# One weight scale for both halves of the first expert, gating due with the second expert

## The chip, the cores and the metric

The kernel runs on one core of a Trainium2 chip. The metric is the device time of one execution in microseconds: 2206.57 us median of three runs (2204.44 to 2206.73) before the change. All rows below come from one execution that was profiled.

## The reference

Attention with a threshold, a gated MLP, and a mixture of eight experts follow each other on 2304 tokens of width 512. The change touches only the mixture:

```
def _moe2_ref(x, w_gate, w1, w2):           # x: 2304 x 512, 8 experts, 1024 wide
    P = np.exp(x @ w_gate - max)            # 2304 x 8
    for _ in range(8):                      # Sinkhorn
        P /= P.sum(1, keepdims=True) + 1e-09
        P /= P.sum(0, keepdims=True) + 1e-09
        P *= N / E
    for e in range(E):
        h = np.maximum(x @ w1[e], 0.0)
        out += P[:, e:e + 1] * (h @ w2[e])
```

## The kernel before

**Numbers.** Every float32 matrix is scaled by a power of two and split into two float16 parts (`split`, line 715: ScalarE copies the high part, line 717, VectorE makes the low one, line 718). A product is six matmuls a pair of blocks: high x high, high x low, low x high, over two blocks of the inner dimension. The scale of a weight needs its largest absolute value: two reductions on VectorE (line 739), a maximum over the partitions by a small matmul (line 131, `all_max`), and five small operations (`pow2_scale`).

**Tiles of the mixture.** Each expert is taken in two halves of 512 hidden columns, so there are 16 half-experts h. A half-expert multiplies by a scheme of seven products instead of eight (sums of blocks are formed first). Tokens stand in three groups g of 768; a unit u is one half-expert on one group, 48 in all. The weights of a half become seven split operands: `weight(which, h, ...)` is a generator that loads 1 MB (line 735), finds the maximum, makes the scale, forms four sums on GpSimd (line 768) and splits seven operands (lines 717, 718).

**Loop.** `first_step(c, j)` is product j (0 to 6) of chain c = 2u + f, six matmuls of 128 x 384 (line 940) into the PSUM banks X and Z, with evictions by ScalarE (`u..a`, `u..c`, `u..b`: lines 950, 957, 960) and VectorE; at j=6 GpSimd makes four sums and four low parts. `second_step` is product j for 128 token pairs, six matmuls of 128 x 256 (line 1011). A step number k counts the first steps in the order of the list `ahead`; 42 steps are a half-expert, and a chain's j=6 comes after the next chain's j=1. Second steps run 21 steps behind, three for each two first steps.

**Order.** TensorE follows the program's order in the loop (`manual_schedule`); on the other engines a planner orders instructions by an estimated time line. `behind()` makes what is issued in it stand behind the loop's last main instruction of the same engine. The generators of the weights are advanced at set steps (`due`, offsets `AT`), for half 1 from k=14 (first weights) and k=34 (second weights).

**Accumulators.** `acc[i]` holds 128 tokens of the output. Half 0 writes or adds its products unscaled, four of seven by ScalarE (line 1023), three by VectorE (1025). Later halves add `ps * coef[h]` (line 1021). `coef[h]` is the gating column times the scales of both weights and of the token. Before half 1's second steps begin, the gating must be done; then `scale_acc` multiplies the 18 accumulators by `coef[0]` (ScalarE, line 1049).

**Gating.** `logits(g)` is 60 small matmuls a group (line 854). Groups 0 and 1 are computed ahead of the last MLP group, group 2 in the loop at k=36. Then `sinkhorn()`, a generator, is advanced every third step: each part ends one column sum over the partitions (two small matmuls, line 892, `cs`) and makes the next row and column sums on VectorE (lines 884 to 897); what is left at the first second step of half 1 runs there.

**x.** The MLP's output is stored as seven operands in DRAM (`x2d`). `load_x(t)` brings operand t into one of ten buffers `xo`, by three transposing DMAs (line 809) the first time, with a store of the result to `x2s` (line 813), and by one plain load (line 815) later. The first fourteen are loaded during the MLP, the last four of them into own buffers `xs10` to `xs13`, which `logits(1)` reads. All these DMAs are on SyncE's queue. Loads in the loop are owed until the step that frees their buffer; in group 2 they are held until its logits are done.

**Start.** The weights 1 of half 0 are made during the second last MLP group. Of the weights 2 of half 0 the load, maximum and scale are there too, the sums and splits are issued just ahead of the loop (`first_w2`), since their tile lies in the pool `pc`, which opens when the MLP's tiles close. An MLP group (lines 523 to 606) has 12 pairs of matmul chains `gv` (line 530) into two PSUM banks, emptied by ScalarE and VectorE, then 72 matmuls `x` (line 561); the last one converts its result in tiles `xf` and `xh` that share the buffers `raw` and `sums` with the weights.

## Time and profile before

| what | value |
|---|---|
| median of three runs | 2206.57 us |
| the profiled execution's own time | 2203.08 us |
| its span, first to last instruction | 2201.3 us |
| mean granted TensorE clock | 0.974 |
| TensorE busy | 1966.6 us, 89% |
| VectorE, ScalarE, GpSimd busy | 73%, 59%, 60% |

PE is TensorE (PEld its weight loads), DVE VectorE, ACT ScalarE, POOL GpSimd, SP SyncE, whose q rows are DMA issues. A busy share is a mean over stages; what a stage is worth is read from its own waits. The clock has two levels; a share between them means that part of the stretch ran at the lower one.

### The profile page before, as it was taken

The page shows a single profiled execution, that of the slowest core. Times are in us where ns is not written, and L with a number is a line of the kernel's source. Part 1 is how long each engine was busy: PE and PEld are TensorE (multiplying, and loading weights), DVE is VectorE, ACT ScalarE, POOL GpSimd, SP SyncE. Part 2 cuts the span into 40 slices and gives each one's busy share as a digit, 9 for nine tenths or more (in the row PEclk, how much of TensorE's full clock was granted, in tenths as well). Part 3 has the DMA queues.
Part 4 walks back from the last instruction along what each step waited for, and adds up shares of the span by engine and source line. Part 5 has one row for each costly group of instructions (what it writes and reads, how often), then busy time and mean ns, then how long its engine had stood idle before and what let it go on. Part 6 is the DMA issues. An engine that isn't in the chain of part 4 may idle for free.

```text
span 2201.3 us, 43806 instructions
## 1 busy us (share of the span) xinstructions
PE 1966.6 (89%) x16464; PEld 1451.6 (66%) x16464; DVE 1614.1 (73%) x3424; ACT 1306.1 (59%) x2804; POOL 1324.6 (60%) x1404
## 2 busy tenths in 40 slices
PE   1358889899998979799999999999999999999998
PEld 0236667766776746577777777677677777776777
DVE  6999677777734247777778787777877787877766
ACT  6878777887743256755555555555555555555552
POOL 1247556675733266557666766776676667667754
PEclk9859899999999989899999999999999999999999
DMA  8885778877737354333343343334333333433332
GB/s 265 207 201 101 174 139 175 163 140 125 131 60 194 79 151 137 109 112 114 122 128 117 117 139 120 113 113 139 110 115 121 126 118 116 139 120 113 94 101 80
DMA packets 372612, 288.36 MB, mean 131 GB/s; under 512 B 286128, under 2 KB 299568, under 8 KB 372400
## 3 DMA queue, kind: packets, MB, share of 16 engines
q1 hardware_dynamic: 371808, 285.55, 49.8%
q8 instruction: 129, 2.11, 0.4%
q14 instruction: 83, 0.68, 0.1%
q0 software_dynamic: 64, 0.00, 0.0%
q10 hardware_dynamic: 528, 0.02, 0.0%
HBM read 193.61 MB, written 21.23 MB: 98 GB/s over the span
## 4 chain that ended last, share of the span: by engine, by line
PE 38%; DVE 15%; POOL 9%; ACT 7%; issue 3%; DMA 2%; SPq 1%; POOLq 0%; DVEq 0%; ACTq 0%
PE P L1011 17%; PE X L940 9%; PE Z L940 6%; DVE w L718 5%; PE gv L530 3%; DVE acc L1021 3%; ACT h L918 2%; PE x L561 2%; DVE h L919 1%; DVE w1m L739 1%; ACT w L717 1%; POOL h L919 1%; DVE w2m L739 1%; DMA xo<-x2d 1%; DVE h L969 1%
## 5 line engine op out<-in xcount | busy, mean ns | idle before, releaser
L1011 PE MATMUL P<-w,h 128*128 128x256 f16 x6048 | 771.2, 273 | 11.0 <-DVE w1mx L133 6.3
L1011 PEld LDWEIGHTS <-h 128*128 128x128 f16 x6048 | 591.8, 98 | 151.6 <-issue 16.2
L940 PEld LDWEIGHTS <-w 128*128 128x128 f16 x4032 | 396.4, 98 | 258.7 <-issue 69.9
L1021 DVE SCALAR_TENSOR_TENSOR acc<-P,coef,acc 128x256 f32<-128x256 f32 x945 | 441.5, 477 | 126.0 <-PE P L1011 116.2
L940 PE MATMUL X<-xo,w 128*128 128x384 f16 x2304 | 441.4, 329 | 53.1 <-ACT u9c L957 7.0
L940 PE MATMUL Z<-xo,w 128*128 128x384 f16 x1728 | 328.8, 327 | 0.0
L304 POOL TENSOR_TENSOR hl<-e,hl 128x512 f16<-128x512 f32 x144 | 171.9, 1193 | 229.6 <-ACT hl L303 150.0
L530 PE MATMUL gv<-xnT,wg 128*128 128x256 f16 x1296 | 168.1, 278 | 8.3 <-DVE u L540 7.1
L530 PE MATMUL gv<-xnT,wv 128*128 128x256 f16 x1296 | 167.8, 276 | 0.0
L330 PE MATMUL pv<-vs,eT 128*128 128x64 f16 (+1 forms) x2240 | 102.9, 201 | 49.7 <-DMA eT<-hl 46.2
L561 PE MATMUL x<-wo,tT 128*128 128x512 f16 x648 | 144.4, 379 | 0.9 <-DVE u L540 0.9
L530 PEld LDWEIGHTS <-wg 128*128 128x128 f16 x1296 | 125.8, 100 | 28.8 <-issue 9.5
L330 PEld LDWEIGHTS <-eT 128*128 128x128 f16 (+1 forms) x2240 | 90.8, 106 | 77.3 <-DMA eT<-hl 60.0
L298 DVE SCALAR_TENSOR_TENSOR e<-S,nt,e 128x576 f32<-128x576 f32 x144 | 116.5, 810 | 32.7 <-ACT e L296 32.3
L530 PEld LDWEIGHTS <-wv 128*128 128x128 f16 x1296 | 126.8, 99 | 16.1 <-issue 0.2
L292 DVE TENSOR_REDUCE nt<-S 128x1 f32<-128x576 f32 x144 | 106.9, 750 | 30.5 <-PE S L282 29.8
L545 POOL TENSOR_TENSOR tT<-u,tT 128x256 f16<-128x256 f32 x108 | 74.3, 689 | 79.6 <-ACT tT L544 79.4
L296 ACT ACTIVATE e<-S,nt,c 128x576 f32<-128x576 f32 x144 | 117.7, 819 | 0.3 <-issue 0.3
L561 PEld LDWEIGHTS <-tT 128*128 128x128 f16 x648 | 62.1, 98 | 71.6 <-issue 1.2
L303 ACT ACTIVATE hl<-e 128x576 f16<-128x576 f32 x144 | 97.1, 676 | 16.1 <-DVE e L298 9.6
L539 DVE SCALAR_TENSOR_TENSOR u<-u,gv 128x256 f32<-128x256 f32 x108 | 44.9, 415 | 76.0 <-ACT u L538 68.9
L282 PE MATMUL S<-kT,qT 128*128 128x288 f16 (+1 forms) x320 | 65.6, 312 | 33.6 <-DVE e L298 24.5
(2539 smaller groups left out, 3607.4 us busy)
## 6 DMA issues: line engine op xcount, KB each, us to landing
xo<-x2s SPq DMA_DIRECT2D x319, 384.0 KB, 3.1
w1r<-in_moe_w_dram SPq DMA_DIRECT2D x16, 1024.0 KB, 5.0
w2r<-in_moe_w_dram SPq DMA_DIRECT2D x16, 1024.0 KB, 5.5
x2s<-xo SPq DMA_DIRECT2D x17, 384.0 KB, 2.7
wgatew<-in_moe_w_gate_dram SPq DMA_DIRECT2D x12, 512.0 KB, 6.0
wo<-in_moe_w_out_dram SPq DMA_DIRECT2D x12, 512.0 KB, 4.1
wvalw<-in_moe_w_val_dram SPq DMA_DIRECT2D x12, 512.0 KB, 4.4
x2d<-xs SPq DMA_DIRECT2D x24, 256.0 KB, 2.8
```

The lines of the kernel that those rows point to most:

```text
L292: V.tensor_reduce(mx, sv, AX.XY, ALU.max)
L296: A.activation(ev, sv, AF.Exp, bias=nt[:, 0:1], scale=st["c2"][:, c : c + 1])
L298: V.scalar_tensor_tensor(ev, sv, nt[:, 1:2], ev, ALU.is_ge, ALU.mult, accum_out=sums[:, slot : slot + 1])
L303: A.activation(hl[:, 0:S], e, AF.Copy)
L304: G.tensor_tensor(hl[:, S + REM :], e[:, 0 : NCH * P], hl[:, 0 : NCH * P], ALU.subtract)
L330: T.matmul(o, lhsT=a, rhs=r, start=n == 0, stop=n == len(mm) - 1)
L530: T.matmul(gv[:, a, :], lhsT=w[:, l, kk, f * P : (f + 1) * P], rhs=xt[:, r * KD + kk, :], start=n == 0, stop=n == 3 * KD - 1,)
L561: T.matmul(ps, lhsT=tT[f][:, l, o : o + P], rhs=wo[:, f, r, :], start=n == 0, stop=n == 3 * KF - 1,)
L718: V.scalar_tensor_tensor(dst[1], src, s, dst[0], ALU.mult, ALU.subtract)
L940: T.matmul(ps, lhsT=w[:, a, l, kk, f * P : (f + 1) * P], rhs=xb[:, r * 2 + kk, :], start=n == 0 and j in (0, 1, 3), stop=n == 5, skip_grou ...
L1011: T.matmul(ps, lhsT=hs[u, ao, f][:, l, jj * P : (jj + 1) * P], rhs=w2[h][:, bo, r, f, :], start=n == 0 and j in (0, 1, 3), stop=n == 5, sk ...
L1021: main[True] = V.scalar_tensor_tensor(y, ps, coef[h][:, i : i + 1], y, ALU.mult, ALU.add)
```

## The change

- Both halves of the first expert get one scale for the first weights and one for the second, from the larger maximum of the two halves. Half 1's weights are loaded once more for that, ahead of the loop, and reduced whole. In the loop half 1 skips its maximum (four empty parts keep the times of the rest).
- With one scale, half 1 adds its products to the accumulators unscaled on VectorE. Coefficients, `scale_acc` and the end of the gating move from the start of half 1's second steps to that of half 2's. `scale_acc` is issued in `behind()`.
- The gating's parts come every sixth step instead of every third.
- All three `logits` are in the loop, at the j=6 of each group's first chain; loads owed are held in each group until its logits are done. The last four early x operands go through three shared buffers `xs` and only to DRAM.
- The second weights of half 0 are made whole ahead of the last MLP group's instructions, in the pool `pb`; second weights of even halves lie in `pb`, of odd ones in `pc`, one buffer each (before: two in `pc`).

```diff
-    def weight(which, h, pool, bufs=1):
+    def load_w(which, h):
         ...
         nc.sync.dma_start(out=r, in_=src.rearrange("(k p) f -> p k f", p=P))
+        return r
+    def largest(dst, r):
+        V.tensor_reduce(dst, r, AX.XY, ALU.max, apply_absolute_value=True)
+    def scale(which, h, m):
+        bits = 3 if which == 1 else 8
+        return pow2_scale(all_max(m, f"w{which}mx"), 1, bits, f"w{which}_{h % 3}")
+    def weight(which, h, pool, r=None):
+        r = load_w(which, h) if r is None else r
         yield
-        m = small([P, 2], f"w{which}m", bufs=2)
-        for a in range(2):
-            V.tensor_reduce(
-                m[:, a : a + 1], r[:, 2 * a : 2 * a + 2], AX.XY, ALU.max,
-                apply_absolute_value=True,
-            )
+        if h >= 2:
+            m = small([P, 2], f"w{which}m", bufs=2)
+            for a in range(2):
+                largest(m[:, a : a + 1], r[:, 2 * a : 2 * a + 2])
+                yield
+            V.tensor_tensor(m[:, 0:1], m[:, 0:1], m[:, 1:2], ALU.max)
             yield
-        V.tensor_tensor(m[:, 0:1], m[:, 0:1], m[:, 1:2], ALU.max)
-        yield
-        ...
+            s, inv = scale(which, h, m[:, 0:1])
+            yield
+        else:
+            s, inv = joint[which]
+            for _ in range(4):
+                yield
...
-    for _ in weight(1, 0, lambda: pb):
-        pass
-    first_w2 = weight(2, 0, lambda: pc, 2)
-    for _ in range(5):
-        next(first_w2)
+    joint = {}
+    for which in (1, 2):
+        m = small([P, 2], f"w{which}m", bufs=2)
+        r = load_w(which, 1)
+        largest(m[:, 1:2], r)
+        r = load_w(which, 0)
+        largest(m[:, 0:1], r)
+        V.tensor_tensor(m[:, 0:1], m[:, 0:1], m[:, 1:2], ALU.max)
+        joint[which] = scale(which, 0, m[:, 0:1])
+        for _ in weight(which, 0, lambda: pb, r=r):
+            pass
...
-            xb = pool.tile([P, KX, TW], F16, tag=f"xs{t}", name=f"xs{u}_{op}")
+            xb = pool.tile([P, KX, TW], F16, tag="xs", name=f"xs{u}_{op}", bufs=3)
...
-    logits(0)
-    logits(1)
...
-        if h > 0:
+        if h > 1:
             main[True] = V.scalar_tensor_tensor(y, ps, coef[h][:, i : i + 1], y, ALU.mult, ALU.add)
-        elif j in (0, 2, 3, 6):
-            A.activation(y, ps, AF.Copy)
+        elif h == 0 and j in (0, 2, 3, 6):
+            main["A"] = A.activation(y, ps, AF.Copy)
         else:
-            V.tensor_tensor(y, ps, y, ALU.add)
+            main[True] = V.tensor_tensor(y, ps, y, ALU.add)
...
-            A.activation(acc[i], acc[i], AF.Copy, scale=coef[0][:, i : i + 1])
+            with behind():
+                main["A"] = A.activation(acc[i], acc[i], AF.Copy, scale=coef[0][:, i : i + 1])
...
-    for _ in first_w2:
-        pass
...
-            if h == 0 and f == 0 and j == 6 and g == NGR - 1:
+            if h == 0 and f == 0 and j == 6:
                 logits(g)
                 gated = u
-            if h != 0 or g < NGR - 1 or gated == u:
+            if h > 0 or gated >= k // 14:
...
-            elif steps is not None and (k - started) % 3 == 0:
+            elif steps is not None and (k - started) % 6 == 0:
...
-                    if hh == 1:
+                    if hh == 2:
...
-                    if hh > 0:
+                    if hh > 1:
                         coef[hh] = coefs(hh)
-                if j == 0 and u // NGR == 1:
+                if j == 0 and u // NGR == 2:
                     m = u * NJ + jj + 1
-                    if m // NJ // NGR == 1:
+                    if m // NJ // NGR == 2:
                         scale_acc(m // NJ, m % NJ)
```

## Rows read from the trace of the kernel before

**Rows 1.** Busy time by stretch: stretch, its us, busy us (instructions) of engines, clock.

```profile
650.00:778.00 128.00, 119.11 (x932) 83.96 (x931) 44.00 (x117) 38.36 (x81) 39.89 (x50) 0.97 0.49 124
778.00:814.20 36.20, 22.98 (x115) 12.40 (x114) 15.25 (x28) 19.05 (x41) 25.68 (x25) 0.81 0.63 161
814.20:1053.36 239.16, 216.25 (x1658) 159.24 (x1656) 180.14 (x386) 142.91 (x306) 153.90 (x147) 0.97 0.40 122
1053.36:1226.25 172.89, 166.58 (x1267) 123.52 (x1265) 134.68 (x267) 94.58 (x196) 117.89 (x112) 1.00 0.39 121
```

**Rows 2.** TensorE's waits, 777 to 935: who for whom, us, times, longest.

```profile
PE cs L892 <- DVE skc L889: 8.4, 3, 5.6
...
PE cs L892 <- DVE acc L1025: 2.6, 1, 2.6
PE P L1011 <- DVE w1mx L133: 1.3, 2, 0.9
```

**Rows 3.** Timeline of TensorE: start, us, what, [idle time before, releaser].

```profile
783.99 5.50 PE L940 MATMUL X<-xo,w 128*128 128x384 f16 x18 [3.93 <-ACT u0c L957]
...
809.83 4.54 PE L940 MATMUL X<-xo,w 128*128 128x384 f16 x18 [6.89 <-ACT u2c L957]
...
920.61 1.14 PE L940 MATMUL X<-xo,w 128*128 128x384 f16 x6
921.58 0.82 PE L1011 MATMUL P<-w,h 128*128 128x256 f16 x6
...
931.65 2.08 PE L940 MATMUL X<-xo,w 128*128 128x384 f16 x6 [6.96 <-ACT u9c L957]
```

**Rows 4.** Groups by line, 784 to 1000: busy us, mean ns, idle before.

```profile
L1021 DVE SCALAR_TENSOR_TENSOR acc<-P,coef,acc 128x256 f32<-128x256 f32 x54 | 25.3, 478 | 9.8 <-PE P L1011 8.0 <-ACT acc L1049 1.0
...
L1049 ACT ACTIVATE acc<-acc,coef 128x512 f32<-128x512 f32 x18 | 11.3, 708 | 0.0
L1025 DVE TENSOR_TENSOR acc<-P,acc 128x256 f32<-128x256 f32 x27 | 11.0, 412 | 0.9 <-PE P L1011 0.6
...
L854 PE MATMUL logits<-wg,xo 128*128 128x16 f16 x60 | 1.7, 169 | 0.0
```

**Rows 5.** Groups of VectorE by line, 848 to 935: gating, first and last.

```profile
L887 DVE TENSOR_TENSOR lg<-lg,skr 128x144 f32<-128x144 f32 x8 | 4.8, 600 | 0.1
...
L894 DVE TENSOR_SCALAR ski<-cs 128x8 f32<-128x8 f32 x8 | 1.3, 159 | 2.4 <-PE cs L892 2.4
```

**Rows 6.** Timeline of GpSimd and ScalarE, 806 to 809.

```profile
806.32 1.57 POOL L768 TENSOR_TENSOR w2s<-w2r,w2s 128x512 f32<-128x512 f32 x1
...
807.93 0.72 ACT L717 ACTIVATE w<-w2s,w_s 128x512 f16<-128x512 f32 x1 [1.91 <-POOL w2s L768]
```

**Rows 7.** Groups by line of VectorE, 650 to 784: weights of half 0.

```profile
L718 DVE SCALAR_TENSOR_TENSOR w<-w1r,w_s,w 128x512 f16<-128x512 f32 x4 | 4.2, 1100 | 0.3 <-ACT w L717 0.3
L718 DVE SCALAR_TENSOR_TENSOR w<-w1s,w_s,w 128x512 f16<-128x512 f32 x3 | 3.9, 1339 | 0.0
...
L739 DVE TENSOR_REDUCE w1m<-w1r 128x1 f32<-128x1024 f32 x2 | 2.3, 1216 | 3.5 <-DMA w1r<-in_moe_w_dram 3.5
...
L718 DVE SCALAR_TENSOR_TENSOR w<-w2r,w_s,w 128x512 f16<-128x512 f32 x3 | 2.2, 746 | 0.3 <-issue 0.3
```

**Rows 8.** Timeline of TensorE in the last MLP groups: three waits.

```profile
680.54 0.55 PE L854 MATMUL logits<-wg,xo 128*128 128x16 f16 x16 [2.44 <-DVE wg L837]
...
689.23 2.06 PE L530 MATMUL gv<-xnT,wg 128*128 128x256 f16 x12 [2.50 <-DVE u L540]
...
731.06 0.27 PE L854 MATMUL logits<-wg,xs 128*128 128x16 f16 x4 [2.01 <-DMA xs<-x2d]
```

**Rows 9.** Timeline of SyncE's queue: transposing loads of group 2, first and last.

```profile
795.81 5.79 SPq L809 DMA_TRANSPOSE xo<-x2d  x4
...
830.00 2.54 SPq L809 DMA_TRANSPOSE xo<-x2d  x2
```

**Rows 10.** DMA issues, 655 to 740: count, median us to landing.

```profile
xo<-x2d SPq DMA_TRANSPOSE x30, 3.0
```

More of the change, by code (lines that the diff above doesn't have):

```diff
@@ L735, in weight @@
         nc.sync.dma_start(out=r, in_=src.rearrange("(k p) f -> p k f", p=P))
-        yield
-        m = small([P, 2], f"w{which}m", bufs=2)
-        for a in range(2):
-            V.tensor_reduce(
-                m[:, a : a + 1], r[:, 2 * a : 2 * a + 2], AX.XY, ALU.max,
-                apply_absolute_value=True,
-            )
-            yield
-        V.tensor_tensor(m[:, 0:1], m[:, 0:1], m[:, 1:2], ALU.max)
-        yield
-        bits = 3 if which == 1 else 8
-        s, inv = pow2_scale(all_max(m[:, 0:1], f"w{which}mx"), 1, bits, f"w{which}_{h % 3}")
-        yield
+        return r
[6 more added lines that the diff above has]
+        r = load_w(which, h) if r is None else r
+        yield
+        if h >= 2:
[4 more added lines that the diff above has]
+            V.tensor_tensor(m[:, 0:1], m[:, 0:1], m[:, 1:2], ALU.max)
+            yield
+            s, inv = scale(which, h, m[:, 0:1])
[4 more added lines that the diff above has]
+                yield
         sm = pb.tile([P, 7, HD], F32, tag="sums", name=f"w{which}s{h}")
@@ L769, in weight @@
             yield
-        w = pool().tile([P, NOP, 2, 2, HF], F16, tag=f"w{which}", name=f"w{which}_{h}", bufs=bufs)
+        w = pool().tile([P, NOP, 2, 2, HF], F16, tag=f"w{which}", name=f"w{which}_{h}")
         for o, a in enumerate((*parts, sm[:, 0], sm[:, 1], sm[:, 2])):
@@ L778, with w_pool @@
     w1, w2, inv1, inv2 = {}, {}, {}, {}
-    def w1_pool(h):
+    def w_pool(h):
         return pb if h % 2 == 0 else pc
-    for _ in weight(1, 0, lambda: pb):
-        pass
-    first_w2 = weight(2, 0, lambda: pc, 2)
-    for _ in range(5):
-        next(first_w2)
+    joint = {}
[9 more added lines that the diff above has]
+            pass
     ORDER = ((0, 0, 0), (1, 1, 1), (2, 5, 4), (3, 4, 2), (4, 3, 5), (5, 2, 6), (6, 6, 3))
@@ L792 @@
     XUSE = [ORDER[j][2] for j in (0, 1, 2, 3, 4, 5, 6)]
-    saved = {}
+    saved = set()
     def load_x(t, pool=None):
@@ L818, in load_x @@
         else:
-            saved[t] = xb
+            saved.add(t)
     pt_cm = tc.tile_pool(name="pt", bufs=1, side="left", reuse_waits="tile")
@@ L827, in x_of @@
         t = u * NOP + XUSE.index(op)
-        return xop[t] if t in xop else saved[t]
+        return xop[t]
     gr = small([P, KD, E], "gr")
@@ L1063 @@
         for which, base in ((1, 42 * (hn - 1) + 14 * (hn == 1)), (2, 42 * (hn - 1) + 21 + 13 * (hn == 1))):
-            n = weight(which, hn, (lambda p: lambda: p)(w1_pool(hn) if which == 1 else pc), which)
+            n = weight(which, hn, (lambda p: lambda: p)(w_pool(hn)))
             for x in AT:
```

## The prediction

> **What bounds the kernel now.** I read the page first (TensorE 89% busy, VectorE 73%, the others about 60%), then the busy time by stretch, then TensorE's waits, then the timelines at the places those two point to. The stretches [rows 1] cut the program at first-step numbers k, counted from the trace: k=2 starts at 778.0 us, k=21 at 814.2, k=126 at 1053.4, k=210 at 1226.2. The last stretch is the steady state: 84 steps in 172.89 us, 2.058 us a step, TensorE idle for 172.89 - 166.58 = 6.3 us. It runs like this to the end, so a change there would count thirteen times over; nothing in the diff alters a step from k=168 (fifth half-expert) on. What can move lies in three earlier stretches.
>
> - Loop, k=21 to 126: 239.16 us for 105 steps, where the steady rate gives 105 x 2.058 = 216.1. Loss 23.0. Named waits of TensorE: 8.4 + 2.6 us for the gating's column sums (`cs`, line 892) and 1.3 for the weight maxima [rows 2], 7.0 for `u9c` on ScalarE [rows 3].
> - Start, k=2 to 21: 36.20 us for 19 steps. A step at full clock starts 0.97 us after the last one (920.61 and 921.58 in [rows 3]), so 18.5 would do. Loss 17.7: 36.20 - 22.98 = 13.2 idle (3.9 for `u0c`, 6.9 for `u2c` [rows 3], 2.4 in shorter ones), the rest the clock: granted 0.81 in this stretch, so part of it at the lower of the two levels (1.2 and 2.4 GHz), and after those two waits 18 matmuls took 5.50 and 4.54 us where three steps need 3.1.
> - MLP, 650 to 778: 128.00 us, TensorE idle 8.9, among it 2.5 at 689 and 2.0 at 731 [rows 1, 8], each with slow matmuls behind it.
>
> **The change, part by part.**
>
> *Gating later and sparser (loop).* Sinkhorn's nine line groups on VectorE sum to 25.1 us for 8 rounds, 3.14 a round ([rows 5] has the first and the last of the nine). One part now comes each 3 steps, 6.2 us at the steady rate. The rest of VectorE's work is (134.68 / 84) = 1.60 us a step [rows 1], 4.8 in three: 4.8 + 3.1 = 7.9 us of work in 6.2 us. That is why TensorE waits at `cs`. With a part every 6 steps there are 12.4 us for 9.6 + 3.1 = 12.7; but between k=36 and 90 the second steps are still those of halves 0 and 1. For half 0 three of seven evictions are on VectorE at 412 ns, against seven at 478 [rows 4], saving 1.5 x (7 x 0.478 - 3 x 0.412)/7 = 0.45 us a step, 2.7 in six. That leaves 10.0 in 12.4 up to k=62, and with the cheaper add of half 1 (412 for 478 ns, 0.6 in six steps) 12.1 in 12.4 after it, less the maxima that are gone. It fits, narrowly in the second part. I let 3 of the 11.0 us of `cs` waits stand: -8.0 (ends: 0, as nothing but the spacing changes, and -11.0). What is late next is an eviction on VectorE, in that 3.
>
> *Scaling of the first expert's sums.* The 18 scalings take 11.3 us of ScalarE [rows 4] and ran as one block after the coefficients were ready; `u9c` stood behind them, 7.0 us. Now they come in half 2, a pair per 128 tokens, each queued behind ScalarE's last loop instruction. ScalarE is at 94.58 of 172.89 us there [rows 1]; a pair of 1.4 us every 9.6 us raises its share from 55 to 69%. Behind a scaling on ScalarE stand evictions of X, for which TensorE waits: I charge 1.5 us for the 18. -7.0 + 1.5 = -5.5 (ends -7.0 and +4: each of nine pairs in the way for its 1.4 us, 12.6, less 7.0, rounded down for what overlaps). The clock behind the two long waits: six matmuls took 2.08 us at 931.65 for 1.14 [rows 3], and some neighbours are as slow; I work with 2.0 to 2.5 us each, -4.5 (ends -6 and 0).
>
> *One scale for both halves.* In the loop the two reductions each of weights 1 and 2 of half 1 and the two maxima over partitions go: 1.3 us of TensorE's wait and 4 x 1.2 us of VectorE (counted above). -1.3.
>
> *Logits of groups 0 and 1* move into the loop: 60 small matmuls each, 1.5 us net a piece (the 1.7 of [rows 4] overlaps its neighbours by a little): +1.5 here, +1.5 in the start. When the big waits go, the steady state's own short ones (6.3 in 84 steps) show in k=21 to 84, where there are now few: +2.
>
> Loop: -8.0 - 5.5 - 4.5 - 1.3 + 1.5 + 2 = -15.8; I take -14, since three items lean on one VectorE estimate.
>
> *Second weights of half 0 (start).* Four sums on GpSimd, and the splits, run inside the start: the last sum ends at 807.9, ScalarE sits 1.91 us for it, then copies, and `u2c`, for which TensorE waits until 809.8, comes behind that [rows 3, 6]. All of that goes into the MLP stretch. GpSimd still has eight operations a chain, so ScalarE still waits for it at times: I leave 2 of 6.9 us, and 0.5 of the 1.5 us of clock behind it; of the 3.9 us for `u0c` 1.2 go, because three splits of 0.75 us stand among VectorE's work at 779 to 781 (the 746 ns in [rows 7]). -4.9 - 1.0 - 1.2 + 1.5 for logits = -5.6 (ends -12, if ScalarE never waits, and +3, if the chain only moves its wait to GpSimd's other eight).
>
> *What the MLP stretch takes on.* Whole-tile reductions of half 1 (two, at 2 x 1.2 us each [rows 7], 4.8 us of VectorE), two more loads of 1 MB, seven splits of weight 2 on VectorE less the three that are in [rows 7], four sums on GpSimd. The stretch has idle room (VectorE 44, ScalarE 38, GpSimd 40 us of 128 [rows 1]), but a matmul group there needs its bank back from VectorE, and seven splits in a row hold VectorE for 8.1 us. In the present trace such a row (672 to 680) held TensorE 2.4 us (680.5 in [rows 8]); I charge 3 for a second and 3.5 for the longer reductions. Off go the logits of two groups (1.7 each, as in [rows 4]) and the wait at 731 with its clock (2.0 + 2.0), which was a transposing load that logits needed early. +6.5 - 3.4 - 4.0 = -0.9 (ends: -8, if VectorE's additions hide, and +14, if 4.8 + 9.4 us of them are exposed whole).
>
> The trace has splits of 746 ns beside an idle GpSimd, and 1100 to 1339 ns while it works [rows 7]. The Trainium skill (SBUF — State Buffer, Who interferes with whom) says that a VectorE instruction with two SBUF inputs and a GpSimd instruction that reads SBUF exclude each other, and the loser stands for the whole of the other; this speaks against moving splits under MLP work that has GpSimd busy. By that rule each of seven splits could wait for a whole sum of 1.3 us, 14 us in place of my 8.1, and the total would be 6 us worse; the trace agrees in kind, with about 0.4 to 0.6 us a split.
>
> *Loads held back.* Loads into x buffers now wait for each group's logits, so five of the seven transposed x tiles of group 2 start at k=22 or just after. Issuing seven took from 795.8 to 832.5 [rows 9], 5.2 us each with the weight loads between, and a transposing load lands 3.0 us after its issue [rows 10]. Five from about 806 are issued by 832 and there by 835; the last is needed at k=36, 806 + 14 x 2.06 = 835. No charge, but no slack (ends 0 and +7, one late tile and the clock). Pools: the second weights alternate between two pools of one buffer, as deep as two buffers in one. 0.
>
> **Sum.** -14 - 5.6 - 0.9 = -20.5. The profiled execution took 2203.08 us (span 2201.3 and 1.8 around it): 2182.6. It lies 3.5 under the median of the runs shown, 2206.57, and the median is what is timed again: about 2186.
>
> **Rivals.**
> - *All covered.* ScalarE and VectorE have room everywhere, no `cs` wait is left and the start runs near TensorE's rate: loop -15.8 - 3 - 1.5 = -20.3, start -5.6 - 2.5 = -8.1, MLP -4, together -32: 2174. For it: no engine but TensorE is over 80% in any stretch of [rows 1]. Against: the queues are in order and these waits came at averages below 80%.
> - *MLP exposed.* The weight work stands whole in the MLP groups: +14 in place of -0.9 leaves -5.6: 2201. For it: the rows of 672 to 680 and the 2.5 us at 689. Against: that stretch has VectorE idle for 84 of 128 us.
> - *Late x tiles*: the transposes held to k=22 run 5 to 7 us late at k=36: 2192. For it the missing slack; against it, a faster start leaves the queue empty earlier.
> - *Not where it says.* The second weights' load waits for a staging buffer that the first weights free, and the x conversion of the last group takes the same buffers; if the splits still land after 778, the start keeps its 17.7 and gains nothing: 2192 to 2196.
> - *Scalings late: slower.* In half 2 each of nine pairs of scalings precedes VectorE's first add of its 128 tokens. VectorE's queue is in order: if the add waits for its pair, 1.4 us [rows 4], the evictions of Z behind it wait, and TensorE with them. With as much again until VectorE has worked off what queued up, and 0.4 of slow clock, that is 3.2 us a pair and 28.8 for nine; it decides from (20.5 + 1.5) / 9 = 2.4 us a pair, and gives 2213. Against it: all but the first pair are issued 128 tokens ahead, some 9.6 us.
>
> **How the numbers follow.** Forecast 0.56, all covered 0.13, MLP exposed 0.14, late x tiles 0.05, not where it says 0.05, scalings late 0.07. A measurement of this kernel tells about 0.2%, 4.4 us, from no change. Within it fall 0.04 of MLP exposed, 0.01 of the weights that stay, 0.02 of late scalings: 0.07. Slower: 0.05 and 0.01 of MLP exposed with a slow clock on top: 0.06. Faster: 0.87. The ends of the terms add up to -42 and +30, but do not come together; 2170 to 2205 leaves out some 0.05 below (all covered, at its far end) and 0.12 above.
>
> **What would show it.** Steps: k=21 to 126 in about 225 us; waits of `cs` for VectorE at most 3 us and none over 2; no block of scalings; k=2 to 21 in about 31 us with no wait of 6 us; the steady stretch at 172.9 us; the stretch before k=2 as long as now, within some 8 us. Wrong: a `cs` wait as large as now (VectorE's load, not spacing, was the cause), a new wait for `xo` at k=30 to 36, waits of `gv` for VectorE in a row in the last MLP group, or a steady stretch that differs at all.

## The result, and the profile after

The changed kernel takes 2182.69 us (median; 2178.03 to 2184.43) against 2205.63 for the kernel before, run beside it on the same chip: a ratio of 0.9893, 95% interval 0.9875 to 0.9911. Measured twice more beside other kernels it came to 0.9901 both times. Its profiled execution took 2184.43 us (span 2182.7) at a granted clock of 0.979, 18.65 us less than the one of before. The forecast was 2186 for the median, and -20.5 between the profiled executions.

The first view is the busy time by stretch of the changed kernel, cut at the same steps as [rows 1] (k=2 is now at 784.3 us, k=21 at 808.2, k=126 at 1034.6).

```profile
650.00:784.00 134.00, 123.80 (x841) 85.82 (x840) 52.33 (x125) 41.79 (x86) 43.98 (x55) 0.92 0.56 142
784.30:808.20 23.90, 20.67 (x176) 12.62 (x175) 10.19 (x22) 16.81 (x38) 18.96 (x21) 1.00 0.67 169
808.20:1034.60 226.40, 214.00 (x1716) 159.56 (x1715) 171.10 (x367) 137.52 (x299) 154.88 (x147) 0.99 0.44 132
1034.60:1208.00 173.40, 166.49 (x1267) 123.51 (x1265) 134.58 (x267) 98.91 (x204) 118.20 (x112) 1.00 0.38 121
```

Read against [rows 1]: the start fell from 36.2 to 23.9 us, the loop from 239.2 to 226.4, the steady stretch stayed nearly (172.9 and 173.4; eight of the 18 scalings, 5.3 us of ScalarE, now lie behind k=126), and the stretch ahead of k=2 grew. A cut at fixed times misleads there, so that stretch is cut at the first matmul of its last two MLP groups:

| stretch | before | after | difference |
|---|---|---|---|
| start of the program to the last MLP group but one | 665.8 | 669.2 | +3.4 |
| last MLP group but one | 60.1 | 68.1 | +8.0 |
| last MLP group, to k=2 | 52.1 | 47.0 | -5.1 |
| start, k=2 to 21 | 36.3 | 23.9 | -12.4 |
| loop, k=21 to 126 | 239.15 | 226.4 | -12.75 |
| k=126 to the end | 1147.9 | 1148.1 | +0.2 |

The first line is not put down to the change: over all the profiled executions below that stretch ended anywhere from 665.5 to 672.3 us (672.1 in a kernel whose only edit lies at k=36 and later), and from 640 us to its end TensorE works without a gap at full clock before and after.

TensorE's waits of the changed kernel follow: who waits for whom, us, times, longest. First the loop (808 to 1035), which answers to [rows 2]:

```profile
PE P L1030 <- DVE w1mx L133: 4.3, 2, 3.1
PE P L1030 <- DVE acc L1044: 2.5, 5, 1.0
PE P L1030 <- DVE ski L913: 2.1, 2, 1.1
PE X L959 <- ACT u11b L979: 1.2, 1, 1.2
PE cs L911 <- DVE acc L1044: 1.2, 1, 1.2
PE X L959 <- ACT u17b L979: 1.0, 1, 1.0
```

The waits of `cs` fell from 11.0 us to 1.2, and the 7.0 for `u9c` [rows 3] is gone. The 2.1 us of `P` for `ski` are new: `ski` is the gating's, and its first instruction empties the PSUM bank of a column sum, which a second step takes next. At the top stands a wait for the weight maximum, 4.3 us in the loop where it was 1.7 (1.3 of it up to 935 us, [rows 2]). Next the start (784 to 808) and the MLP (655 to 784):

```profile
...
PE X L959 <- ACT u1c L976: 1.0, 1, 1.0
...
PE gv L530 <- DVE u L540: 8.3, 3, 3.7
PE w1mxp L131 <- DVE xm L570: 1.9, 1, 1.9
```

**The start**, in TensorE's timeline; the rows answer to 783.99 and 809.83 of [rows 3].

```profile
786.62 3.08 PE L959 MATMUL X<-xo,w 128*128 128x384 f16 x18 [0.23 <-ACT u0c L976]
...
805.17 3.16 PE L959 MATMUL X<-xo,w 128*128 128x384 f16 x18 [2.02 <-ACT u2c L976]
```

The wait for `u0c` went from 3.93 to 0.23 us and the 18 matmuls behind it from 5.50 to 3.08; `u2c` went from 6.89 to 2.02 and from 4.54 to 3.16.

**The last MLP group but one**, TensorE's timeline. A `gv` chain of 12 takes 1.47 us where nothing disturbs it.

```profile
688.62 2.72 PE L530 MATMUL gv<-xnT,wg 128*128 128x256 f16 x12 [3.19 <-DVE u L540]
691.14 2.77 PE L530 MATMUL gv<-xnT,wv 128*128 128x256 f16 x12
...
705.86 2.72 PE L530 MATMUL gv<-xnT,wg 128*128 128x256 f16 x12 [3.66 <-DVE u L540]
```

Two chains after each wait run at about half speed, at the lower of the clock's two levels (granted 0.50 from 688.62 to 693.70 and from 705.86 to 710.90, 0.85 in the group on the mean). VectorE's timeline shows what TensorE's banks waited for:

```profile
681.87 3.72 DVE L718 SCALAR_TENSOR_TENSOR w<-w1r,w_s,w 128x512 f16<-128x512 f32 x4
685.52 2.06 DVE L718 SCALAR_TENSOR_TENSOR w<-w1s,w_s,w 128x512 f16<-128x512 f32 x3
688.17 0.74 DVE L540 SCALAR_TENSOR_TENSOR u<-u,gv 128x256 f32<-128x256 f32 x2
```

Seven splits in a row hold VectorE from 681.87 to 687.58; the evictions `u`, which free a bank, stand behind them in the queue, and TensorE starts again at 688.62. The same happens at 699 to 705 with the second weights' seven. The third wait for `u` (1.4 us) and the one for `xm` (1.9) lie at 672 to 675.5 us, behind the first weights' whole-tile reductions.

**The new wait in the loop**, TensorE and then VectorE:

```profile
966.41 0.22 PE L131 MATMUL w1mxp<-ident,w1m 128*128 128x128 bf16 x1
969.77 1.66 PE L1030 MATMUL P<-w,h 128*128 128x256 f16 x12 [3.14 <-DVE w1mx L133]
```

```profile
965.16 0.29 DVE L916 TENSOR_TENSOR lg<-lg,ski 128x144 f32<-128x144 f32 x1
...
966.64 1.92 DVE L925 TENSOR_SCALAR coef<-lg,w_i 128x18 f32<-128x18 f32 x2
...
969.44 0.28 DVE L133 TENSOR_REDUCE w1mx<-w1mxp 128x1 f32<-128x128 f32 x1
```

The small matmul of the maximum of weights 1 of half 3 is done at 966.63. The reduction of its result stands on VectorE behind the coefficients of two half-experts, and the next second step on TensorE waits for its bank. The program issues these coefficients at the first second step of half 2 (k=105); VectorE has them earlier, right behind the gating's last instruction at 965.16. With a part every sixth step that last part is issued at k=90, next to the maximum of half 3, which is due at k=94.

### The profile page after: what moved, and what is told of

Its sections match the earlier page's. It is cut to its first block, busy times and chain, and to the rows that moved or that the text cites. A ratio compares the mean times of both kernels' runs of the same rounds, so it can differ in the third digit from the quotient of the medians.

```text
span 2182.7 us, 43793 instructions
## 1 busy us (share of the span) xinstructions
PE 1967.9 (90%) x16462; PEld 1453.4 (67%) x16462; DVE 1606.6 (74%) x3404; ACT 1305.3 (60%) x2804; POOL 1321.1 (61%) x1404
## 4 chain that ended last, share of the span: by engine, by line
PE 42%; DVE 16%; POOL 8%; ACT 7%; issue 4%; DMA 1%; SPq 0%; DVEq 0%; POOLq 0%; ACTq 0%
PE P L1030 17%; PE X L959 9%; PE Z L959 6%; PE gv L530 5%; DVE w L718 5%; PE x L561 3%; DVE acc L1040 3%; ACT h L937 2%; ACT w L717 2%; DVE h L938 2%; DVE w1m L740 1%; POOL h L938 1%; DVE w2m L740 1%; DVE h L988 1%; DMA eT<-hl 1%
## 5 line engine op out<-in xcount | busy, mean ns | idle before, releaser
L1030 PEld LDWEIGHTS <-h 128*128 128x128 f16 x6048 | 591.2, 98 | 157.6 <-issue 22.9
L1040 DVE SCALAR_TENSOR_TENSOR acc<-P,coef,acc 128x256 f32<-128x256 f32 x882 | 411.8, 477 | 113.3 <-PE P L1030 105.4
L530 PEld LDWEIGHTS <-wg 128*128 128x128 f16 x1296 | 128.7, 101 | 36.4 <-issue 14.4
L296 ACT ACTIVATE e<-S,nt,c 128x576 f32<-128x576 f32 x144 | 117.7, 819 | 0.3 <-issue 0.3
L282 PE MATMUL S<-kT,qT 128*128 128x288 f16 (+1 forms) x320 | 66.3, 314 | 33.0 <-DVE e L298 23.7
```

What stands on the lines that cost most here:

```text
L296: A.activation(ev, sv, AF.Exp, bias=nt[:, 0:1], scale=st["c2"][:, c : c + 1])
L530: T.matmul(gv[:, a, :], lhsT=w[:, l, kk, f * P : (f + 1) * P], rhs=xt[:, r * KD + kk, :], start=n == 0, stop=n == 3 * KD - 1,)
L1030: T.matmul(ps, lhsT=hs[u, ao, f][:, l, jj * P : (jj + 1) * P], rhs=w2[h][:, bo, r, f, :], start=n == 0 and j in (0, 1, 3), stop=n == 5, sk ...
L1040: main[True] = V.scalar_tensor_tensor(y, ps, coef[h][:, i : i + 1], y, ALU.mult, ALU.add)
```

## The experiments

All ratios are to the kernel before, run on the same chip, with 95% intervals. The last four columns, in us, are from each profiled execution.

| kernel | ratio | MLP group but one | last group | start | loop |
|---|---|---|---|---|---|
| before | 1 | 60.1 | 52.1 | 36.3 | 239.2 |
| changed | 0.9893 [0.9875, 0.9911] | 68.1 | 47.0 | 23.9 | 226.4 |
| e_after2 | 0.9901 [0.9881, 0.9921] | 65.6 | 52.1 | 25.5 | 226.4 |
| e_after3 | 0.9901 [0.9884, 0.9919] | 65.5 | 48.7 | 25.5 | 226.5 |
| e1_every3 | 0.9939 [0.9926, 0.9951] | 66.3 | 52.1 | 25.5 | 231.0 |
| e3_block | 0.9937 [0.9923, 0.9950] | 65.0 | 48.7 | 23.9 | 231.3 |
| e5_before6 | 1.0036 [1.0022, 1.0051] | 59.8 | 53.5 | 36.4 | 246.9 |
| e2_w2_late | 0.9917 [0.9904, 0.9930] | 60.4 | 53.3 | 29.5 | 224.8 |
| e10_three | 0.9891 [0.9874, 0.9907] | 64.4 | 48.5 | 27.3 | 224.7 |
| e6_no_half1 | 0.9885 [0.9867, 0.9902] | 62.3 | 53.2 | 23.9 | 228.0 |
| e4_spread | 0.9912 [0.9899, 0.9926] | 56.2 | 59.3 | 23.9 | 227.4 |
| e7_spread2 | 0.9885 [0.9868, 0.9901] | 56.4 | 54.1 | 25.5 | 224.8 |
| e8_store | 0.9881 [0.9863, 0.9899] | 64.0 | 47.0 | 25.5 | 224.8 |
| e9_both | 0.9827 [0.9809, 0.9845] | 49.1 | 47.1 | 23.9 | 226.5 |

**The loop: spacing (e1_every3).** The changed kernel with the old spacing of the gating's parts.

```diff
-            elif steps is not None and (k - started) % 6 == 0:
+            elif steps is not None and (k - started) % 3 == 0:
```

> The changed kernel with the gating's parts every third step again; they are still due only with half 2. Theory (the spacing removed the column-sum waits): the waits of cs for VectorE come back to some 8 to 11 us with a slow clock behind, k=21 to 126 takes 235 to 238 us for 226.4, time about 2193 against 2182.7. Rival (the waits came from half 1's maxima and the deadline, not from the spacing): cs waits stay under 3 us and the time within 3 us of 2182.7.

TensorE's waits in its loop:

```profile
PE cs L911 <- DVE skc L908: 7.8, 2, 6.6
PE cs L911 <- DVE acc L1044: 2.5, 1, 2.5
```

The waits of [rows 2] are back almost to the figure (10.3 us against 11.0), and the ratio rises to 0.9939. So these waits came from the spacing, with all else as in the changed kernel. But the loop is only 4.6 us longer, where 9 to 12 were expected: with the wide spacing go waits that it brings, 2.6 us for `w1mx`, 2.1 for `ski` and 2.3 for `acc`. TensorE's idle time rises by 1.8 us, and its busy time by 2.8 at a granted clock of 0.97 for 0.99. The spacing is worth 4.6 us of the loop, not the 9.1 by which `cs` differs.

This run also says what makes the new wait for `w1mx`; VectorE and TensorE:

```profile
941.65 1.06 DVE L925 TENSOR_SCALAR coef<-lg,w_i 128x18 f32<-128x18 f32 x1
```

```profile
982.53 1.47 PE L1030 MATMUL P<-w,h 128*128 128x256 f16 x12 [0.38 <-DVE w1mx L133]
```

Here the gating is through at 922 us, the coefficients run at 924 to 943, and the maximum of half 3, at 982, costs 0.38 us in place of 3.14. So it is the end of the gating, moved by the spacing, that puts them in its way.

**The loop: the deadline (e5_before6).** The reverse: the kernel before with the wide spacing alone.

```diff
-            elif steps is not None and (k - started) % 3 == 0:
+            elif steps is not None and (k - started) % 6 == 0:
```

> The kernel before with one thing changed: parts of the weight work are let out at every sixth step and not at every third, each half's scale and due time left as they were. Theory (the wide spacing is open only because the gating and scaling are due with the second expert, so that the parts have 40 steps more): here the parts left over at the end of the first expert's steps run in one lump ahead of its first matmuls of the second layer, TensorE waits there for several us, and the loop k = 21 to 126 is longer than the 239.2 us of before by 5 to 30 us; median 2211 to 2235. Rival (spacing alone brings the gain, as e1_every3, which took it away, cost 9 us): the waits of cs for skc go (8.4 us) and the loop takes 230 to 233; median 2197 to 2200.

The "parts of the weight work" of this expectation are the gating's parts, as the edit shows. The kernel is slower than before, and its loop 7.7 us longer. TensorE's timeline at the point where half 1's second steps begin:

```profile
914.84 0.59 PE L892 MATMUL cs<-skc,ones 128*128 128x8 f32 x2 [4.73 <-DVE skc L889]
...
930.34 0.60 PE L892 MATMUL cs<-skc,ones 128*128 128x8 f32 x2 [2.67 <-DVE skc L889]
```

The five rounds left over run in one lump, 17.8 us of waits. So the one scale, which costs reductions and a load, earns its place here by moving the due time; the spacing can't be had without it.

**The loop: order of the scalings (e3_block).** They are issued where they were, not behind the loop's own ScalarE work.

```diff
-            with behind():
-                main["A"] = A.activation(acc[i], acc[i], AF.Copy, scale=coef[0][:, i : i + 1])
+            A.activation(acc[i], acc[i], AF.Copy, scale=coef[0][:, i : i + 1])
```

> The changed kernel with the 18 scalings issued without an order behind the loop's instructions. Theory (the order kept them from running as one block): they run in blocks of 3 to 6 us on ScalarE near k=104 to 110, one wait of TensorE of 5 to 8 us with slow clock behind: 7 to 9 us slower, about 2191. Rival (with the coefficients known early the planner spreads them itself): no wait over 2 us, time within 3 us of 2182.7.

ScalarE's timeline, and the wait that it makes for TensorE:

```profile
968.06 6.25 ACT L1068 ACTIVATE acc<-acc,coef 128x512 f32<-128x512 f32 x10 [2.22 <-DVE coef L926]
```

```profile
PE X L959 <- ACT u13b L979: 3.7, 1, 3.7
```

The block is back, and an eviction behind it holds TensorE 3.7 us, in the place of `u9c`'s 7.0 (5 to 8 were expected). The loop is 4.9 us longer than the changed one. So the move to half 2 alone takes the wait from 7.0 to 3.7 us, and the place in the queue takes the rest.

**The start: sums and four splits (e2_w2_late).** The generator of the second weights of half 0 is made ahead of the last MLP group and run only ahead of the loop. The three splits that need no sum went into the MLP by themselves (699.5 to 701.8 us), since their tile is in `pb`.

```diff
-        for _ in weight(which, 0, lambda: pb, r=r):
-            pass
+        half0 = weight(which, 0, lambda: pb, r=r)
+        if which == 1:
+            for _ in half0:
+                pass
...
+    for _ in half0:
+        pass
     BEHIND = 7
```

> The changed kernel with the sums and splits of half 0's second weights issued after the last MLP group, just ahead of the loop, as before; tile still in pb. Theory (ScalarE stood behind GpSimd's sums in the start, and the MLP stretch pays for the move): k=2 to 21 takes 34 to 37 us for 23.9, the MLP stretch gets 4 to 6 us shorter; net 6 to 9 us slower, about 2190. Rival (the start got faster for other reasons: logits gone, coefficients gone): k=2 to 21 stays under 27 us and the time falls to about 2178.

TensorE's waits in its start, then a sum on GpSimd and ScalarE's queue ahead of `u2c`:

```profile
PE X L961 <- ACT u2c L978: 5.6, 1, 5.6
...
PE X L961 <- ACT u0c L978: 0.2, 1, 0.2
```

```profile
805.07 1.57 POOL L783 TENSOR_TENSOR w2s<-w2r,w2s 128x512 f32<-128x512 f32 x1
```

```profile
806.68 0.72 ACT L717 ACTIVATE w<-w2s,w_s 128x512 f16<-128x512 f32 x1 [0.81 <-POOL w2s L783]
808.08 0.52 ACT L939 ACTIVATE h<-u1s 128x384 f16<-128x384 f32 x1 [0.67 <-POOL u1s L997]
808.51 0.47 ACT L978 ACTIVATE u2c<-X 128x384 f32<-128x384 f32 x1
```

The wait for `u2c` is back (5.6 us, before 6.9): ScalarE stands for the sums and for what runs behind them on GpSimd, and `u2c` behind that. The wait for `u0c` is not back. The start takes 29.5 us, 5.6 above the first profiled execution of the changed kernel (4.0 above the other two) and 6.8 below before. That is between the theory's 34 to 37 us and the rival's 27: this part of the second weights explains a third to a half of the start's gain. The MLP group but one takes 60.4 us, where three executions of the changed kernel take 65.5 to 68.1. But the last group takes 53.3, with a wait of 3.2 us for `u`, so both together (113.7 us for 114.2 to 117.7) don't price the move.

**The start: the three splits (e10_three).** Now only those three are put back on VectorE ahead of `u0a`, where they stood.

```diff
-        for o, a in enumerate((*parts, sm[:, 0], sm[:, 1], sm[:, 2])):
+        todo = list(enumerate((*parts, sm[:, 0], sm[:, 1], sm[:, 2])))
+        if which == 2 and h == 0:
+            todo = [todo[o] for o in (1, 4, 5, 6, 0, 2, 3)]   # the last three wait
+        for o, a in todo:
...
+    with tc.issue_after(places["V"].ins):      # the last reduction of the last MLP group
+        for _ in half0:
+            pass
...
-            V.tensor_tensor(st["A"], Z, st["A"], ALU.add)
+            with tc.issue_after(places["split"].ins) if (u, f) == (0, 0) else ExitStack():
+                V.tensor_tensor(st["A"], Z, st["A"], ALU.add)
```

> The changed kernel with one thing put back: the low parts of the three second-weight splits of half 0 that need no sum stand on VectorE just ahead of the addition u0a, where they stood in the kernel before (779 to 781 us there). The sums and the other four splits stay in the MLP groups. Theory (these three hold up u0a, hence ScalarE's u0c, for which TensorE waits at a lowered clock): the wait of X for u0c is back at 2 to 4 us with slow matmuls behind it, u2c waits no more than 2 us, and k = 2 to 21 takes 28 to 32 us against 23.9 to 25.5; the loop stays at 225 to 228. Rival (the 1.2 us that the prediction charged for them is all they cost, and the rest of the start's gain has another cause, as the logits or the loads that left it): 25 to 26.7 us, with no wait for u0c over 1.5 us. The total, 2181 to 2193, can't tell the two apart.

27.3 us, short of the theory's 28 to 32 and over the rival's 26.7, and no wait for `u0c`. ScalarE's order differs; first the kernel before, then this one:

```profile
782.05 0.52 ACT L953 ACTIVATE u0a<-u0a 128x384 f32<-128x384 f32 x1 [6.38 <-DVE u0a L952]
782.48 0.67 ACT L581 ACTIVATE xf<-x,xm 128x512 f32<-128x512 f32 x1
783.05 0.51 ACT L918 ACTIVATE h<-u0a 128x384 f16<-128x384 f32 x1
783.46 0.48 ACT L957 ACTIVATE u0c<-X 128x384 f32<-128x384 f32 x1
```

```profile
781.88 0.49 ACT L986 ACTIVATE u0c<-X 128x384 f32<-128x384 f32 x1 [5.28 <-PE X L968]
784.08 0.52 ACT L982 ACTIVATE u0a<-u0a 128x384 f32<-128x384 f32 x1 [1.71 <-DVE u0a L981]
...
793.56 0.52 ACT L946 ACTIVATE h<-u0s 128x384 f16<-128x384 f32 x1 [2.66 <-POOL u0s L1005]
793.99 0.47 ACT L986 ACTIVATE u1c<-X 128x384 f32<-128x384 f32 x1
```

Before, ScalarE's relu of `u0a` waited for VectorE's add behind the three splits, and `u0c` stood fourth in that queue. Here `u0c` stands ahead of that relu; the conversion of the last group's x slipped instead, GpSimd's sums with it, and TensorE waited 2.93 us for `u1c`, with 18 matmuls of 4.54 us behind. Against the changed kernel's 23.9 to 25.5 us the three splits cost 1.8 to 3.4 us here, about their own 2.1 us and not clearly more. What they cost in the old order this run can't say, and the theory is not shown.

**MLP: is it the look at half 1? (e6_no_half1).** Its two loads and reductions are left out; the scales come from half 0 alone, so this kernel leaves out half 1's part of the maxima.

```diff
-        r = load_w(which, 1)
-        largest(m[:, 1:2], r)
...
-        V.tensor_tensor(m[:, 0:1], m[:, 0:1], m[:, 1:2], ALU.max)
```

> The changed kernel without the look at half 1 ahead of the loop: both scales come from half 0's maximum alone, so two loads of 1 MB and two whole-tile reductions are left out. Theory (the last but one MLP group pays for VectorE's longer work): that group falls from 68 to 62 to 64 us, time 4 to 6 us under the changed kernel's. Rival (the splits in rows are the price, not the reductions): the group stays at 66 to 68 us, time within 2 us.

62.3 us in the group but one, 3 to 6 less than the changed kernel's three executions, and a total (0.9885) that the intervals don't tell from 0.9893. The group came out as the theory said, but the 4 to 6 us in the total did not show. The price of looking at half 1 is small, and this run can't give it better.

**MLP: weights among the groups' own work (e4_spread, e7_spread2).** Each reduction (in halves) and each split is bound behind the work of one of the group's 12 matmul pairs, the first weights in the last group but one and the second in the last. In e4_spread the second weights' loads are issued just ahead of the last group, in e7_spread2 a group earlier.

```diff
+    def put(n, j, f):          # one part of the weights behind pair f of group j
+        with ExitStack() as es:
+            for ins in places[j, f]:
+                es.enter_context(tc.issue_after(ins.ins))
+            next(n, None)
...
+    for f in range(KF):
+        put(n1, LASTJ - 1, f)
+    next(n2)                   # e7_spread2: the loads; e4_spread has this line further down
...
-    mlp_out(NTL // 2 - 1, mlp_in(NTL // 2 - 1), pb)
+    tT8 = mlp_in(LASTJ, lambda f: put(n2, LASTJ, f))
```

> The changed kernel with half 0's weights spread: reductions in halves, one part behind each of the 12 pairs of matmul chains, the first weights in the last but one MLP group, the second in the last. Theory (the MLP stretch loses to rows of splits that hold VectorE while matmuls wait for their banks): the waits of gv for VectorE, 8.3 us, shrink under 2, slow clock goes, the last but one group falls from 52.5 to 35 to 42 us: 10 to 15 us faster than the changed kernel, 2168 to 2173. Rival (the stretch is set by its DMA queue, on which the stores and transposes stand in one line): the group stays over 48 us and the time within 4 us of 2182.7.

> As e4_spread, but the second weights' loads are issued ahead of the x loads, so that no reduction stands in VectorE's queue for a load. Theory (rows of splits and a late load were the price): the 9.65 us wait goes, no wait of gv over 4.1 us is left, both groups together 104 to 110 us where the changed kernel took 115; time 2170 to 2176. Rival (stores of x behind transposing loads on SyncE's queue set these groups): waits of 3 to 4 us with ScalarE standing for a store stay in both groups, together 112 to 116 us, time 2180 to 2186.

The group but one fell to 56 us in both, not to the 35 to 42 expected. And in e4_spread a load came late, so that the last group took 59.3 us; SyncE's queue, VectorE and TensorE:

```profile
733.01 1.07 SPq L740 DMA_DIRECT2D w2r<-in_moe_w_dram  x2
```

```profile
738.88 1.22 DVE L745 TENSOR_REDUCE w2m<-w2r 128x1 f32<-128x1024 f32 x1 [11.40 <-DMA w2r<-in_moe_w_dram]
```

```profile
740.94 2.72 PE L532 MATMUL gv<-xnT,wg 128*128 128x256 f16 x12 [9.65 <-DVE u L542]
```

The loads stood behind transposing loads on SyncE's queue, the reduction waited in VectorE's queue with the evictions behind it, and TensorE 9.65 us. With the loads earlier that is gone, and both groups together take 110.5 us, where the theory said 104 to 110 and the rival 112 to 116. A second mechanism shows; e7_spread2, ScalarE, then SyncE's queue, then TensorE:

```profile
688.32 0.42 ACT L605 ACTIVATE xs<-x2t 128x256 f16<-128x256 f32 x1 [5.98 <-DMA x2d<-xs]
```

```profile
684.57 1.23 SPq L861 DMA_TRANSPOSE xo<-x2d  x1
685.89 0.52 SPq L607 DMA_DIRECT2D x2d<-xs  x1
```

```profile
690.06 2.72 PE L532 MATMUL gv<-xnT,wg 128*128 128x256 f16 x12 [4.42 <-DVE u L542]
```

ScalarE's copy into `xs` waits for the store that empties the buffer, the store stands behind the transposing loads, and the next `gv` eviction stands behind the copy.

**MLP: the stores by another queue (e8_store).** The stores of `x2d` of two groups are issued by GpSimd.

```diff
-            nc.sync.dma_start(
+            (G if j in (NTL // 2 - 3, NTL // 2 - 2) else nc.sync).dma_start(
```

> The changed kernel with the x stores of the two MLP groups before the last issued from GpSimd's queue instead of SyncE's, where they stand behind transposing loads. Theory (rows of splits are the price in the last but one group): that group stays over 62 us, and only the wait in the last group, where there is one, goes: time 2178 to 2184. Rival (the queue sets both groups): the last but one group falls under 60 us and the time to 2170 to 2176.

The last group takes 47.0 us and TensorE waits in it for nothing; as one execution of the changed kernel has that too, the store's part shows only in the next run. The group but one stays at 64.0: the blocks of splits are still there. By itself this can't be told from the changed kernel in the total (0.9881).

**Both (e9_both)** holds e7_spread2's and e8_store's edits.

> The changed kernel with both earlier remedies for its last two MLP groups: the second weights of the first half stand one reduction or one split behind each matmul pair of the group (as in e7_spread2), and the stores of x2d of the last groups but one go from GpSimd's queue (as in e8_store). Theory (two separate waits: the reductions in VectorE's order in the last group but one, the stores behind transposing loads in the last): the last group but one takes 56 to 57 us as in e7_spread2 (68.1 in the changed kernel) and the last 47 to 48 as in e8_store (54.1 in e7_spread2), so the MLP stretch to k = 2 takes 110 to 113 us against 118.1 and 118.6 with one of them, and the median is about 2175 to 2178. Rival (one cause, both edits take away the same wait, and the time returns elsewhere): the stretch stays at 117 to 119 us and the median at 2181 to 2183.

2167.01 us, 0.9827 [0.9809, 0.9845], where the changed kernel beside it on the same chip has 0.9901 [0.9884, 0.9919]: faster than both. Busy time of its last two groups:

```profile
669.40:718.50 49.10, 49.10 (x376) 36.51 (x375) 25.86 (x62) 18.20 (x38) 22.78 (x28) 1.00 0.94 216
718.50:765.60 47.10, 47.10 (x363) 35.31 (x362) 24.74 (x55) 18.18 (x38) 22.70 (x29) 1.00 0.42 122
```

TensorE is busy without a gap at full clock, with 25.9 us of VectorE's work in the first of them. The theory gave 56 to 57 us for that group, as in e7_spread2, and it took 49.1: the store's wait (4.42 us at 690.06 in e7_spread2, with two slow chains behind it) had cost that group too. The two groups take 96.2 us together, which shows what the others lose: the changed kernel 115.1 - 96.2 = 18.9 us (18.0 and 21.5 in its other two executions), with one remedy 14.3 (e7_spread2) and 14.8 (e8_store). Either wait alone leaves most of the loss standing.

**Controls (e_after2, e_after3).** The changed kernel again.

> The changed kernel once more, for its spread and its waits in a second profiled execution. Theory (the last MLP group's wait of 1.5 to 3.3 us seen in three of the variants, and the time at which attention ends, differ from one execution to the next): median 2180 to 2186; the loop's stretch 226.4 and the start 23.9 as before within 0.5 us, the MLP groups off by up to 5 us. Rival (the variants' own edits made that wait): the last group as short as in the first profile, 47 us up to k=2.

> The changed kernel once more, beside the two above: median 2181 to 2187, the last group but one 64 to 69 us and the last 47 to 52.

Loop and steady stretch repeat to 0.1 us. The last MLP group took 47.0, 52.1 and 48.7 us, the start 23.9, 25.5 and 25.5 (23.9 was expected). The wait in the last group was thus not made by the variants' edits. The loop takes 224.7 to 228.0 us in variants whose edits lie ahead of it, so a difference there of under 2 us says little. Single profiles tell edits of the MLP apart by several us at best, and the totals there are judged by the intervals.

## Why the prediction was right, and which steps were not

The total came out as forecast: -18.65 us for -20.5 between the profiled executions. The mechanisms of the loop were right. That the total lies so near is in part luck, since errors cover each other: against the forecast the start gave 6.8 us more, and the MLP 3.8 less, the loop 1.25 less, and 3.4 were lost in a stretch that can't be put down to the change. One of the prediction's own signs of being wrong came, waits of `gv` for VectorE in a row (8.3 us) in the last MLP groups.

- **Loop, -14: right, -12.75.** The `cs` waits gave -9.8 where -8.0 was forecast; with the 2.1 us for `ski` that came for them it is -7.7. `u9c` gave -7.0. e1_every3 brings back the one almost whole and e3_block 3.7 us of the other, at 4.6 and 4.9 us of the loop. TensorE's busy time fell by 2.25 us with 1.7 of logits added, so the clock gave back 3.9 (forecast 4.5). Its idle time fell by 22.9 - 12.4 = 10.5 in all, so the other short waits took 1.6 more, where +2 and +1.5 stood. **The step that failed is "-1.3" for the maxima**: they cost 2.6 more (4.3 for 1.7). The 1.3 was misread to begin with, as two rows of the kernel before show:

```profile
821.35 0.81 PE L1011 MATMUL P<-w,h 128*128 128x256 f16 x6 [0.38 <-DVE w1mx L133]
...
886.45 0.81 PE L1011 MATMUL P<-w,h 128*128 128x256 f16 x6 [0.90 <-DVE w1mx L133]
```

Only the first, 0.4 us, is for half 1; the second is for half 2, whose maximum stays. And half 3's went from 0.38 to 3.14 us, since the end of the gating, with two sets of coefficients behind it, came to lie just where it is due. I counted the maxima that go and did not look at what the moved gating stands ahead of.

- **Start, -5.6: too small, -12.4** (-10.8 in the other two executions of the changed kernel). The terms for `u2c` hold: -4.9 forecast, 6.89 - 2.02 = -4.9 measured, and -1.4 of clock for -1.0. The logits cost 1.5 as said. **The step that failed is "of the 3.9 us for `u0c` 1.2 go"**: 3.7 went, and 2.4 of slow matmuls behind it (5.50 to 3.08), -6.1 in all; another 1.4 were short waits of `u1` that I left standing. In the kernel before, VectorE's `u0a` stands behind the three splits (3.52 us after k=2, 0.81 in the changed kernel), and `u0c` stands on ScalarE behind the relu of `u0a`; I had charged part of the splits' own duration and nothing for that queue. How much of the 6.1 is theirs stays open, as e10_three's order of ScalarE was another and its cost came out at 1.8 to 3.4 us.
- **MLP, -0.9: too small a cost, +2.9.** The last group gave -5.1 where -1.7 for the logits and -4.0 for the wait stood [rows 8]. But that gain is not firm: a like wait, now for the store behind the transposing loads, is there in e_after2 (52.1 us) and gone in e9_both. **The step that failed is "+6.5" for the weight work**: it cost 8.0 + 1.7 = +9.7 in the last group but one. TensorE's idle time there rose by 3.3 us, half of what I charged; the rest, 4.7 + 1.7 = 6.4 us, is the clock. I charged the waits and, here alone, no slow matmuls behind them. In e_after2 and e_after3 the cost comes to 7.2 and 7.1 us, 3.1 and 4.4 of it clock, so the amount varies, and the clock is in it each time.
- **Loads held back, 0: right.** No execution shows a wait for `xo` in the start or the loop. The rival of late x tiles is refuted, as are late scalings (waits on ScalarE in the loop of 1.2 and 1.0 us) and a start that keeps its weights. "MLP exposed" was partly true: 18.9 us were there to lose, but 12.6 of such loss stood before already (112.2 less 3.4 of logits less 96.2).
- **Splits beside GpSimd.** Seven splits of the second weights took 5.2 us (745 and 741 ns each on the mean), under my 8.1 and far under the 14 of the other rule, with next to nothing on GpSimd beside them. Of the first weights' seven, one took 1.64 us, from 682.63 to 684.27, while GpSimd worked from 682.12 to 683.72. In e9_both one took 1.62 us from 739.66, beside a sum from 739.46 to 740.73, which agrees with what the Trainium skill says (SBUF — State Buffer, Who interferes with whom) of the loser that stands until the other is through. The price is real, but it falls on the splits that meet an instruction of GpSimd, not on all.

## What to carry to other kernels

Where work is moved under another stage, look in every in-order queue at what stands directly behind the moved instruction: a row of splits, a reduction whose load is late, or a copy whose buffer a store must empty each held up the eviction that TensorE's next bank needed, at an average load of VectorE of 48% (33.0 of 68.1 us in the changed kernel's group). Charge each such wait with the slow matmuls behind it, here 2.0 to 2.5 us for a wait of 3.2 to 9.7, and let out the work one piece behind each eviction. Work made sparser ends later: look at what its end then stands ahead of. Two waits in one stretch can cover for each other: take both away before judging either.

## What was not expected of the hardware

- The same wait of 2.02 us at `u2c` is followed by 18 matmuls of 3.16 us in one execution of the changed kernel and 4.76 in another (3.08 behind the wait of 0.23 us): the granted clock there is 1.00 in the one and 0.63 in the other, so it falls behind some waits of that length and not behind others.
- The waits of 3.19 and 3.66 us in the MLP group but one are each followed by two `gv` chains of 2.72 to 2.77 us where 1.47 is normal, at a granted clock of 0.50, so 2.5 us are lost on top of each.
- With the stores issued by GpSimd the last group goes from 54.1 us (e7_spread2) to 47.1 (e9_both), and no loss on GpSimd shows: beside TensorE at 100% it was busy 22.7 of 47.1 us in e9_both.
